# Staging the last V groups of a load phase in free buffers, and running four projection groups on the first weight half-piece

## The chip, the cores and the metric

The kernel runs on 1 core of one Trainium2 chip. The metric is device time in microseconds (us) of one execution; smaller is better. The time before was 859.42 us, the median of 3 runs (859.0 to 860.41). The span that a profile shows is about 1.7 us shorter than the time of the same run.

Engines are named as the profile names them: PE is TensorE (matmul), PEld its weight loads, ACT is ScalarE, DVE is VectorE, POOL is GpSimd, SP is SyncE, which issues nearly all DMAs here. "L463" is line 463 of the kernel. The change adds three lines early in the file, so that L699 of before is L702 of after, L512 is L515, L656 is L659, and so on.

## The reference, cut to what matters

A segment-recurrent attention layer over 64 segments, and then a gated MLP. Only the attention's loop and its weights matter here.

```python
for s in range(n_seg):                       # 64 segments of 32 rows, strictly one after another
    h = concat([mem, x[s]])                  # 8 memory rows + 32 rows
    q, k, v = h @ Wq, h @ Wk, h @ Wv         # 512 -> 32 heads x 128
    p = softmax(mask(q @ k.T * scale))
    o = (p @ v) @ Wo                         # needs every row of Wo
    mem = o[:8]                              # next segment's memory
    outs.append(o[8:])
... x + attention, then layernorm, gelu, spatial gating, output projection
```

The kernel computes what does not depend on the memory ahead of the loop: the projections Q, K and V of some rows of x, for whole chunks of 16 segments ("chunk 0", "chunk 1", ...). Chunks 0 and 1 are done in a load phase, while the weights arrive: 4 MB each of Wq, Wv, Wk and Wo. Then step 0 of the loop starts, then step 1, and so on, with no slack between the steps. For this document the load phase ends at about 54 us, and step 1 starts at about 64 us.

## The kernel before

Operations are recorded in program order. Each names the tokens (tiles) that it reads and writes, and a scheduler derives the semaphore waits: a write to a token waits for all readers of its old contents, and a DMA that stores a tile is such a reader. Each engine is given its own operations in the recorded order.

Weights come in pieces of eight heads (1 MB). The first piece of Wq is cut in two halves, so that PE can start sooner:

```python
def load_w(mi, hq):                          # mi 0, 1, 2: Wq, Wk, Wv; hq: piece 0..3
    ...
    if mi == 0 and hq == 0:
        cm = c0 + 4 * DH
        sp(lambda e, c0=c0: e.dma_start(ws[:, :, c0:cm], wr[:, :, c0:cm]), writes=["W0"])
        c0 = cm
    sp(lambda e: e.dma_start(ws[:, :, c0:c1], wr[:, :, c0:c1]), writes=[("W", mi, hq)])
```

A Q/K group `i` of a chunk is 16 matmuls of 128x128 into one PSUM bank; `hhs` names which quarter groups to run (L463). The V groups are L498. Their eviction (ACT or DVE) writes a staging buffer, which SP then stores to DRAM (`vext_d`):

```python
def qkx_mm(ck, i, bank, hhs=range(4)):
    ...
    for hh in hhs:
        wt = "W0" if i < 2 and hh < 2 else ("W", mi, q // 2)
        for dc in range(DC):
            pe(... e.matmul(ps[:, bank, hh * 128:(hh + 1) * 128], lhsT=ws[...], rhs=hTe[:, ck % 3, dc, :], ...),
               reads=[("hTe", ck % 3, dc // 2), wt], writes=[PB(bank)])

def vx_evac(ck, n, bank, eng="act"):
    if ck == 1 and n < 4:
        t, tok = (hbuf, xo)[n // 2][:, n % 2, :], [(("h", "xo")[n // 2], n % 2)]
    elif ck < 2:
        t, tok = part[:, n, :], [("part", n, 0), ("part", n, 1)]
    else:
        t, tok = Vs[:, 0, :], [("Vs", 0)]
    ...                                      # ACT or DVE: PSUM bank -> t
    sp(lambda e: e.dma_start(dst, t...), reads=tok, writes=[("vext", ck, n)])
```

So V groups 4 to 7 of chunk 1 use the same four buffers (`part` 4 to 7) as those of chunk 0, and their evictions wait until those stores have been done.

The start of the load phase, and its end:

```python
for hp in range(2):                          # start: chunk 0 on both halves of piece 0, then chunk 1
    for i in range(2):
        qkx_mm(0, i, 2 + i, (2 * hp, 2 * hp + 1))
    if hp == 0:
        xe_halves(1, 1, (0, 1))              # x transposes of chunk 1
qkx_evac(0, 0, 2, "act")
qkx_evac(0, 1, 3, "dve")
for i in range(2):
    qkx_mm(1, i, 4 + i)
    qkx_evac(1, i, 4 + i, ("act", "dve")[i])
...
for i in range(2, 8):                        # rest of Q
    for ck in range(2):
        start_group(qkx_mm, qkx_evac, ck, i)
...                                          # V groups of chunk 0, V groups 0..3 of chunk 1, load_wo(0)
load_wo(1)
for j in range(2):
    load_vx(j)                               # reads vext_d back: waits for stores of chunk 0
for i in range(8, 12):                       # first half of K
    ...
for n in range(4, 8):
    start_v(1, n)                            # V groups 4..7 of chunk 1
    if n % 2 == 1:
        load_wo(n // 2)                      # the third and the last Wo piece
for i in range(12, 16):                      # second half of K
    ...
```

`start_group` cycles through four PSUM banks. In a step the output product reads all of Wo, and `V_evac` writes the tile `V_sb`:

```python
def Wo(cbs, bank, d0, d1):                   # L699
    for c, b in cbs:
        for g in range(4):
            h = 16 * b + 4 * c + g
            pe(... rhs=w_o[:, h, d0:d1] ..., reads=[("cT", c, b), ("Wo", h // 8)], writes=[PB(bank)])

def V_evac(b, eng, gs=(0, 4)):               # L654 (ACT), L656 (DVE)
    dst, src = V_sb[:, b, 128 * gs[0]:128 * gs[1]], ps[...]
    tok = [("V", b, g) for g in range(*gs)]
    ...
```

## Time and profile before

| what | value | from |
|---|---|---|
| time | 859.42 us (859.0 to 860.41, 3 runs) | runs |
| PE busy | 845.2 us, 98% of the span | page, busy times |
| first V matmul (start of V groups) | 22.86 us | PE timeline |
| step 0 starts / step 1 starts | 54.46 / 64.69 us | PE timeline |
| Wo pieces 2, 3, 4 (counted from 1) landed | 51.66 / 58.01 / 62.79 us | completion records of the DMAs |

From the page of the kernel before, the busy times of the span, and the two DMA rows over 40 equal slices of it (21.5 us each; a digit is tenths of the DMA engines' time):

```profile
PE 845.2 (98%) x22497; PEld 427.6 (50%) x18920; DVE 506.4 (59%) x1312; ACT 471.7 (55%) x1359; POOL 156.3 (18%) x423
...
DMA  8983222213041211322241313243231690032101
GB/s 303 373 254 73 71 73 74 65 42 86 26 93 32 77 37 49 82 67 58 69 86 44 81 40 97 68 84 71 47 69 39 192 280 3 1 111 89 46 13 41
```

PE bounds the whole. But the first three slices, some 64 us, are also full of DMA. That is where both of the idle times that the change aims at lie. The busy times by stretch show them (columns: stretch, its length, busy us and instructions of each engine, granted clock, DMA share, GB/s):

```profile
35.00:54.00 19.00, 17.64 (x314) 15.40 (x313) 7.19 (x10) 6.61 (x10) 7.88 (x32) 1.00 0.95 306
54.00:64.00 10.00, 9.63 (x309) 5.08 (x251) 5.86 (x15) 6.03 (x18) 1.55 (x4) 1.00 0.75 242
```

PE lacks 19.00 - 17.64 = 1.36 us between 35 and 54 us. The PE timeline names the gaps (columns: start, duration, engine, line, operation, count; in brackets the idle time before the group and what ended it):

```profile
6.83 1.19 PE L463 MATMUL f_ps<-f_hTe,f_arena 128*128 128x128 bf16 x16 [0.16 <-ACT f_hTe L443]
7.85 0.39 PE L408 MATMUL f_ps<-f_ident,f_xn 128*128 128x128 bf16 x4
9.29 13.65 PE L463 MATMUL f_ps<-f_hTe,f_arena 128*128 128x128 bf16 x240 [1.05 <-DMA f_arena<-in_A_Wq_dram]
...
45.67 1.07 PE L463 MATMUL f_ps<-f_hTe,f_arena 128*128 128x128 bf16 x16
48.10 6.43 PE L463 MATMUL f_ps<-f_hTe,f_arena 128*128 128x128 bf16 x112 [1.36 <-DVE f_part L512]
54.46 0.40 PE L289 MATMUL f_ps<-f_arena,f_hT 128*32 128x512 bf16 x4
...
60.84 0.27 PE L290 MATMUL f_ps<-f_arena,f_hT 128*32 128x256 bf16 x1 [0.37 <-issue]
...
62.46 1.86 PE L699 MATMUL f_ps<-f_arena,f_cT 128*32 128x256 bf16 x56
```

The gap before 9.29 waits for the second half of the first weight piece, the gap before 48.10 for a bank that DVE had not yet emptied.

Why DVE was late is in the list of waits of the first 75 us (columns: who, for what, us in total, times, longest):

```profile
ACT f_part L510 <- DMA vext_d<-f_part: 5.3, 2, 3.1
DVE f_part L512 <- DMA vext_d<-f_part: 4.7, 2, 4.4
```

Both evictions waited for older stores out of `part`. And the SP timeline shows what sets the end of the Wo loads: SP stands at the read-back of V (`f_Vx`) from 45.70 to 50.07, and issues the last Wo piece at 53.72.

```profile
45.70 4.37 SPq L520 DMA_DIRECT2D f_Vx<-vext_d  x4
...
52.05 0.47 SPq L823 DMA_DIRECT2D f_arena<-in_A_Wo_dram  x1
...
53.72 0.57 SPq L823 DMA_DIRECT2D f_arena<-in_A_Wo_dram  x1
```

That last piece landed at 62.79, and step 0's Wo matmuls (L699), which need it, run from 62.46.

### The profile page before, as it was taken

To read this page: it belongs to the slowest core of one execution; us is meant where nothing else is said; L and a number is where in the kernel's file an instruction comes from. 1 tells how busy PE (TensorE), PEld (TensorE's weight loads), DVE (VectorE), ACT (ScalarE), POOL (GpSimd) and SP (SyncE) were. 2 spreads that over 40 slices of the span, in tenths; PEclk is the share of its full clock that TensorE was granted. 3 is DMA by queue.
4 is the path that set the end of the run, shared out by engine and by line. 5 is a ranking of instruction groups with operands and counts; after the bars stand their busy time and mean duration, and the time that the engine had idled before them with its cause. 6 is when DMAs were issued, how large, how long until landed. Compare 5 with 4: busy or idle time off the path is not lost.

```text
span 859.1 us, 45449 instructions
## 1 busy us (share of the span) xinstructions
PE 845.2 (98%) x22497; PEld 427.6 (50%) x18920; DVE 506.4 (59%) x1312; ACT 471.7 (55%) x1359; POOL 156.3 (18%) x423
## 2 busy tenths in 40 slices
PE   8999999999999999999999999999999999999997
PEld 8664445454444544445444454444544444444443
DVE  3546666666666666666666666666665564463443
ACT  3445666666666666666666666666666655400000
POOL 0711212121212112121211212121111132100000
PEclk9999999999999999999999999999999999999999
DMA  8983222213041211322241313243231690032101
GB/s 303 373 254 73 71 73 74 65 42 86 26 93 32 77 37 49 82 67 58 69 86 44 81 40 97 68 84 71 47 69 39 192 280 3 1 111 89 46 13 41
DMA packets 114713, 75.25 MB, mean 88 GB/s; under 512 B 70728, under 2 KB 100560, under 8 KB 114512
## 3 DMA queue, kind: packets, MB, share of 16 engines
q1 hardware_dynamic: 114224, 72.06, 30.6%
q8 instruction: 164, 2.69, 1.3%
q14 instruction: 37, 0.30, 0.1%
q10 hardware_dynamic: 288, 0.20, 0.1%
HBM read 39.46 MB, written 20.58 MB: 70 GB/s over the span
## 4 chain that ended last, share of the span: by engine, by line
PE 96%; DMA 2%; DVE 1%; issue 0%; SPq 0%; ACT 0%; DVEq 0%
PE f_ps L289 30%; PE f_ps L699 13%; PE f_ps L290 13%; PE f_ps L1148 11%; PE f_ps L749 3%; PE f_ps L498 3%; PE f_ps L463 3%; PE f_ps L664 3%; PE f_ps L1222 3%; PE f_ps L1110 3%; PE f_ps L613 3%; PE f_ps L1141 3%; PE f_ps L593 1%; PE f_ps L670 1%; DMA f_arena<-in_A_Wq_dram 1%; DMA vext_d<-f_part 1%
## 5 line engine op out<-in xcount | busy, mean ns | idle before, releaser
L289 PE MATMUL f_ps<-f_arena,f_hT 128*32 128x512 bf16 (+1 forms) x5120 | 352.9, 337 | 1.1
L290 PE MATMUL f_ps<-f_arena,f_hT 128*32 128x256 bf16 (+1 forms) x3072 | 214.6, 308 | 0.4 <-issue 0.4
L289 PEld LDWEIGHTS f_ps<-f_arena,f_hT 128*32 128x32 bf16 x5120 | 120.5, 96 | 169.0 <-issue 86.0
L557 ACT ACTIVATE f_Tst<-f_ps 128x512 bf16<-128x512 f32 (+1 forms) x320 | 149.8, 510 | 57.1 <-PE f_ps L289 53.4
L699 PE MATMUL f_ps<-f_arena,f_cT 128*32 128x256 bf16 x4096 | 130.0, 274 | 1.3 <-ACT f_cT L684 1.1
L636 POOL TENSOR_TENSOR f_E_sb<-f_R_sb,f_E_sb 128x64 bf16<-128x64 f32 x128 | 48.0, 375 | 374.4 <-ACT f_R_sb L628 374.4
L565 DVE STREAM_TRANSPOSE f_QT<-f_Tst 128x256 uint32<-128x256 uint32 x128 | 57.1, 446 | 94.5 <-ACT f_Tst L557 94.5
L699 PEld LDWEIGHTS f_ps<-f_arena,f_cT 128*32 128x32 bf16 x4096 | 90.2, 94 | 35.3 <-ACT f_cT L684 22.9
L1148 PE MATMUL f_ps<-f_arena 128*128 128x512 bf16 x448 | 100.6, 379 | 0.0
L656 DVE TENSOR_SCALAR f_V_sb<-f_ps 128x512 bf16<-128x512 f32 (+1 forms) x128 | 70.6, 552 | 40.9 <-PE f_ps L289 40.9
L686 DVE TENSOR_SCALAR f_cT<-f_ps 128x160 bf16<-128x160 f32 x256 | 65.1, 317 | 36.4 <-PE f_ps L670 36.4
L711 ACT ACTIVATE f_part<-f_ps 128x256 bf16<-128x256 f32 x128 | 49.2, 384 | 59.2 <-PE f_ps L699 56.0
L684 ACT ACTIVATE f_cT<-f_ps 128x160 bf16<-128x160 f32 x256 | 57.1, 309 | 36.9 <-PE f_ps L670 36.9
L1148 PEld LDWEIGHTS f_ps<-f_arena 128*128 128x128 bf16 x448 | 43.7, 98 | 52.8
L565 DVE STREAM_TRANSPOSE f_KT<-f_Tst 128x128 uint32<-128x128 uint32 (+1 forms) x192 | 66.0, 356 | 2.7
L624 ACT ACTIVATE f_R_sb<-f_ps 128x160 f32<-128x160 f32 x128 | 39.0, 304 | 33.6 <-PE f_ps L290 26.5
L1154 DVE TENSOR_TENSOR f_arena<-f_ps,f_arena 128x512 f32<-128x512 f32 x28 | 19.3, 690 | 54.4 <-PE f_ps L1148 52.4
L606 ACT ACTIVATE f_E_sb<-f_ps 128x224 bf16<-128x224 f32 x128 | 45.7, 357 | 0.0
L632 DVE TENSOR_TENSOR f_E_sb<-f_R_sb,f_E_sb 128x160 bf16<-128x160 f32 x128 | 44.8, 350 | 0.0
L628 ACT ACTIVATE f_R_sb<-f_R_sb 128x160 f32<-128x160 f32 x128 | 42.6, 333 | 2.0
L749 PE MATMUL f_ps<-f_arena,f_cTx 128*32 128x512 bf16 x512 | 40.6, 380 | 0.0
L289 PE MATMUL f_ps<-f_arena,f_hTe 128*32 128x512 bf16 x512 | 39.2, 382 | 0.0
(116 smaller groups left out, 1023.0 us busy)
## 6 DMA issues: line engine op xcount, KB each, us to landing
wT_d<-f_wst SPq DMA_DIRECT2D x32, 256.0 KB, 3.7
f_arena<-wT_d SPq DMA_DIRECT2D x32, 256.0 KB, 4.6
f_arena<-in_A_Wv_dram SPq DMA_DIRECT2D x4, 1024.0 KB
f_arena<-in_A_Wk_dram SPq DMA_DIRECT2D x4, 1024.0 KB, 15.7
f_arena<-in_A_Wo_dram SPq DMA_DIRECT2D x4, 1024.0 KB
f_Vx<-vext_d SPq DMA_DIRECT2D x128, 32.0 KB
f_arena<-in_A_Wq_dram SPq DMA_DIRECT2D x3, 1024.0 KB
vext_d<-f_Vs SPq DMA_DIRECT2D x16, 128.0 KB
```

What stands on the lines that cost most here:

```text
L289: return e.matmul(out, lhsT=lhsT, rhs=rhs, start=start, stop=stop, skip_group_check=True, tile_position=pos)
L290: return e.add_instruction(mybir.InstMatmult(name=nc.get_next_instruction_name(), engine=mybir.EngineType.PE, ins=[e.lower_ap(rhs), e.lowe ...
L557: act(lambda e: e.activation(out=st_.rearrange("p (hp i r) -> p hp i r", i=32, r=2), in_=ps[:, bank, 0:64 * np_].rearrange("p (hp r i) -> ...
L565: dve(lambda e: e.transpose(out=dst, in_=src), reads=tok, writes=[(nm, b, k) for k in halves(b, p0, np_)])
L636: pool(lambda e: e.tensor_tensor(out=ev, in0=rv, in1=ev, op=ALU.mult), reads=[("R", b), ("Ex", b)], writes=[("Ex", b)])
L656: dve(lambda e: e.tensor_scalar(out=dst, in0=src, scalar1=VSC, scalar2=None, op0=ALU.mult), reads=[PB(bank)], writes=tok)
L684: act(lambda e: e.activation(out=dst, in_=src, func=ACT.Copy, scale=UNSC), reads=[PB(PVB[c])], writes=tok)
L686: dve(lambda e: e.tensor_scalar(out=dst, in0=src, scalar1=UNSC, scalar2=None, op0=ALU.mult), reads=[PB(PVB[c])], writes=tok)
L699: pe(lambda e, h=h, g=g, i=i, b=b, c=c: e.matmul(ps[32 * g:32 * g + 32, bank, 0:d1 - d0], lhsT=cTh[:, i, 8:40], rhs=w_o[:, h, d0:d1], star ...
L711: act(lambda e: e.activation(out=part[:, s % 8, d0:d1], in_=ps[:, bank, 0:d1 - d0], func=ACT.Copy), reads=[PB(bank)], writes=[("part", s % ...
L749: pe(lambda e, h=h, g=g, i=8 * qr + bg: e.matmul(ps[32 * g:32 * g + 32, WXB, :], lhsT=cTx[:, rb % 2, i, :], rhs=w_o[:, h, :], start=(i < 4 ...
L1148: pe(lambda e: e.matmul(ps[:, bank, 0:TB], lhsT=z2[:, sc, fb * 128:(fb + 1) * 128], rhs=wTb[tb % 2][:, :, sc, :], start=(sc == 0), stop=(s ...
```

## The change

It has two parts. (a) At the start, both chunks run their first two groups on the first half piece (`hhs` 0 and 1), with the x transposes of chunk 1 between, and only then the second half: PE gets 16 more matmuls before it needs the second half. (b) V groups 4 to 7 of chunk 1 are staged in `Vs` and `V_sb`, which no store is reading then, so their evictions need not wait.

```diff
     def vx_evac(ck, n, bank, eng="act"):
         if ck == 1 and n < 4:
             t, tok = (hbuf, xo)[n // 2][:, n % 2, :], [(("h", "xo")[n // 2], n % 2)]
-        elif ck < 2:
+        elif ck == 1:
+            t = (Vs, V_sb)[n // 2 - 2][:, n % 2, :]
+            tok = [("Vs", n % 2)] if n < 6 else [("V", n % 2, g) for g in range(4)]
+        elif ck == 0:
             t, tok = part[:, n, :], [("part", n, 0), ("part", n, 1)]
 ...
-    for hp in range(2):
+    qkx_mm(0, 0, 2, (0, 1))
+    xe_halves(1, 1, (0, 1))
+    qkx_mm(0, 1, 3, (0, 1))
+    for i in range(2):
+        qkx_mm(1, i, 4 + i, (0, 1))
+    for ck in range(2):
         for i in range(2):
-            qkx_mm(0, i, 2 + i, (2 * hp, 2 * hp + 1))
-        if hp == 0:
-            xe_halves(1, 1, (0, 1))
-    qkx_evac(0, 0, 2, "act")
-    qkx_evac(0, 1, 3, "dve")
-    for i in range(2):
-        qkx_mm(1, i, 4 + i)
-        qkx_evac(1, i, 4 + i, ("act", "dve")[i])
+            qkx_mm(ck, i, 2 + 2 * ck + i, (2, 3))
+            qkx_evac(ck, i, 2 + 2 * ck + i, ("act", "dve")[i])
```

No work is added or removed, and the order in which SP issues DMAs is the same.

## The prediction

> **What bounds the kernel.** Over the whole span TensorE does: the page has PE busy 98% and PE 96% of the chain that ended last, clock 0.9 or better in every slice. In the first 62 us a second limit runs beside it: windows from 10 to 50 us show DMA share about 1.05 and 334 to 385 GB/s. Weights land in issue order ([...] the trace agrees: 1 MB pieces land one after another, 2.7 us apart). PE waits there for data that no reordering of PE brings sooner.
>
> **What the change does.** It adds and removes no work; SyncE's issue order stays.
>
> (a) Start. PE waits 1.05 us, 8.24 to 9.29, for the rest of the first weight piece (PE timeline). The change puts 16 matmuls of chunk 1 there, about 0.9 us (240 took 13.65 us). But the matmuls after need the second 1 MB piece, whose semaphore is full at 11.94 us. Before, the matmul with that wait was already held a little: evictions come every 0.89 us, but after 0.97 at 12.25, and a new run of weight loads starts at 11.98. After, PE has 32 matmuls (1.8 us) left at 9.29, finishes near 11.1, and waits 0.9 us. Gain at 12 us: about 0.
>
> (b) V groups 4 to 7 of chunk 1. Their evictions waited for older stores out of the same buffers (list of waits: ACT 5.3, DVE 4.7 us on DMA vext_d<-f_part), and PE idled 1.36 us before 48.10 for a bank. With Vs and V_sb as staging this goes; PE reaches step 0 near 53.1 instead of 54.46. But step 0 needs all four pieces of Wo. The last lands at 62.79, and PE got there at 62.75: its weight loads pause until 62.84. That landing hangs on SyncE's issue order and the queue: Vx loads wait for stores landing at 48.21, then stores, Wo piece 3 issued at 52.05 (lands 58.01), piece 4 at 53.72. None of that waits for what the change makes earlier. So PE arrives near 61.4 and waits about 1.35 us. Step 0's V evictions now wait for the last two staged stores (58.45, 58.84) and are wanted near 58.3 and 59.2: up to 0.2 us, hidden under the Wo wait.
>
> **Sum.** 0.9 + 1.36 = 2.3 us of visible idle is removed (0.27%); I expect 0 to 0.2 us to survive, as both idles lie ahead of a later deadline set by DMA. From 63 us on both kernels should run alike.
>
> **Predicted: 859.3 us**, 8 in 10 between 858.2 and 860.3 (three runs of before spread 1.4 us). Chances: faster by over 2% 0.005, within 2% 0.99, slower by over 2% 0.005.
>
> **What would show it.** Right: the PE gap before 9.29 shrinks to 0.2 us and one of about 0.9 ends near 11.95; no ACT or DVE wait on vext_d stores between 43 and 48 us; step 0 starts near 53.1; then over 1 us of idle in its Wo matmuls, ending near 62.85; step 1 starts near 64.7 in both. Wrong: step 1 near 63.3 ((b) kept, about 858.0) or 62.4 (both kept, 857.1).
>
> **What would make it wrong.** The last Wo piece landing earlier, if SyncE or the queue goes faster once the stores' data is ready earlier; landing times shifting by some tenths; or the staged stores landing later than step 0 wants V_sb, by more than the Wo wait hides.

## The result, and the profile after

| | median us | lowest to highest | runs |
|---|---|---|---|
| before | 859.21 | 858.67 to 860.41 | 4 |
| after | 859.13 | 858.80 to 859.79 | 4 |

The ratio after/before is 0.9998, with a 95% interval of 0.9981 to 1.0015: the same. Ratios in this document are the mean time of one kernel's runs over that of the other's runs of the same rounds, so they are not quite the ratio of the medians quoted.

The busy times by stretch, after:

```profile
35.00:54.00 19.00, 19.00 (x343) 16.04 (x331) 7.80 (x11) 7.16 (x10) 7.82 (x32) 1.00 0.96 299
54.00:64.00 10.00, 8.93 (x304) 4.69 (x248) 5.74 (x16) 5.79 (x18) 1.40 (x4) 1.00 0.73 239
```

The gap between 35 and 54 us is gone (19.00 of 19.00), and 10.00 - 8.93 = 1.07 us of idle time stands between 54 and 64 us, where there had been 0.37. PE's timeline after:

```profile
7.20 0.51 PE L463 MATMUL f_ps<-f_hTe,f_arena 128*128 128x128 bf16 x6 [0.28 <-DVE f_hTe L445]
7.54 0.39 PE L408 MATMUL f_ps<-f_ident,f_xn 128*128 128x128 bf16 x4
7.77 7.16 PE L463 MATMUL f_ps<-f_hTe,f_arena 128*128 128x128 bf16 x119
15.43 7.38 PE L463 MATMUL f_ps<-f_hTe,f_arena 128*128 128x128 bf16 x129 [0.49 <-DMA f_arena<-in_A_Wq_dram]
...
45.54 7.32 PE L463 MATMUL f_ps<-f_hTe,f_arena 128*128 128x128 bf16 x128
52.79 0.40 PE L289 MATMUL f_ps<-f_arena,f_hT 128*32 128x512 bf16 x4
...
59.48 0.27 PE L290 MATMUL f_ps<-f_arena,f_hT 128*32 128x256 bf16 x1 [0.69 <-issue]
...
61.10 0.51 PE L702 MATMUL f_ps<-f_arena,f_cT 128*32 128x256 bf16 x11
61.99 1.48 PE L702 MATMUL f_ps<-f_arena,f_cT 128*32 128x256 bf16 x45 [0.37 <-DMA f_arena<-in_A_Wo_dram]
```

Read it from the top. The wait before 9.29 is gone, but a new one stands at 15.43, for the third 1 MB piece of Wq; the first V matmul comes at 22.73 instead of 22.86. The group at 45.54 now runs its 128 matmuls without the gap in the middle, and step 0 starts at 52.79, 1.67 us earlier than before. Then that lead shrinks: the "issue" gap is 0.69 us instead of 0.37, and the Wo matmuls break off for 0.37 us until the last Wo piece has landed (61.94). Step 1 starts at 63.80, 0.89 us earlier than before in this pair of profiles; the timed runs show no such difference.

The waits of the first 75 us, after, which answer to those shown of before:

```profile
PE f_ps L290 <- issue: 0.7, 1, 0.7
...
PEld f_ps L702 <- DMA f_arena<-in_A_Wo_dram: 0.6, 1, 0.6
...
DVE f_V_sb L659 <- DMA vext_d<-f_V_sb: 0.5, 1, 0.5
```

No eviction waits for a store out of `part` any more. In their place stand three shorter waits, all in step 0: the issue gap, the wait for Wo, and a wait of DVE for a staged store out of `V_sb`.

In the chain that ended last, SP and the Wo load now stand where PE's own work stood before (start, duration, what):

```profile
49.72 0.46 SPq L517
...
52.92 9.02 DMA f_arena<-in_A_Wo_dram
...
61.99 1.48 PE f_ps L702 x45
```

So the idle time has moved to where DMA sets the pace. Three things could be holding step 0 there, and the profile alone does not separate them: the last Wo piece, the staged stores, and whatever "issue" is.

### The profile page after: what moved, and what is told of

Its sections match the earlier page's. It is cut to its first block, busy times and chain, and to the rows that moved or that the text cites. A ratio compares the mean times of both kernels' runs of the same rounds, so it can differ in the third digit from the quotient of the medians.

```text
span 858.1 us, 45452 instructions
## 1 busy us (share of the span) xinstructions
PE 844.5 (98%) x22504; PEld 426.0 (50%) x18920; DVE 506.2 (59%) x1312; ACT 471.3 (55%) x1359; POOL 156.1 (18%) x423
## 3 DMA queue, kind: packets, MB, share of 16 engines
q8 instruction: 164, 2.69, 1.3%
## 4 chain that ended last, share of the span: by engine, by line
PE 94%; DMA 3%; DVE 1%; SPq 1%; issue 0%; ACT 0%
PE f_ps L289 30%; PE f_ps L702 13%; PE f_ps L290 13%; PE f_ps L1150 11%; PE f_ps L752 3%; PE f_ps L498 3%; PE f_ps L1224 3%; PE f_ps L667 3%; PE f_ps L1112 3%; PE f_ps L616 3%; PE f_ps L1143 3%; PE f_ps L463 2%; PE f_ps L596 1%; DMA f_arena<-in_A_Wq_dram 1%; DMA f_arena<-in_A_Wo_dram 1%; PE f_ps L673 1%
```

## The experiments

### What "issue" is

Before the experiments, one reading of the traces. Take PE's matmuls and weight loads in their order of start and number them; the first is number 2, as the trace has two instructions of PE's sequencer before it. In every execution that has the "issue" gap of step 0 it falls between number 1984 and number 1985, and when there is a second one, between 2240 and 2241; later ones can be seen before 2753 and 3265. These numbers are multiples of 256 apart. The page counts "q8 instruction: 164, 2.69" as packets and MB on a DMA queue of its own: 2.69 MB over 164 packets is 16 KB each, and PE's 41417 matmuls and weight loads (22497 and 18920 on the page of before) over 164 packets are 253 to a packet, near the 256 between the gaps. Where there is a gap at number 1985, it ends 1.23 to 1.41 us after such a packet has ended (before: packet 58.51 to 59.48, PE resumes at 60.84; after: 57.28 to 58.25, PE resumes at 59.48). From these figures the gap is read here as PE waiting for its next page of 256 instructions; the profile itself names no releaser but "issue".

The packet starts 2.3 us (before) and 2.75 us (after) after PE has entered the page ahead of it, while Wo pieces are moving; on the next six, quieter pages of before it is 0.6 to 1.3 us (for example: page entered at 64.56, packet at 65.89; 73.39 and 74.18).

In the experiments "stall" is the time from the start of number 1984 to that of number 1985, with 0.65 us before and 0.97 us after. (The page's 0.37 and 0.69 are shorter, because they count from the modelled end of the matmul before.) Likewise "Wo wait" is the time at the first matmul that needs the last Wo piece (number 2128): 0.65 us after. The table below leaves out the second stall, from number 2240 to 2241, just before step 1's first instruction: it is 0.35 us before, 0.12 after, 0.74 in a_only and after_vxlate, 0.47 in b_only and after_nowo3, 0.19 in after_again, 0.20 in before_again, and nothing in the others.

### The theories

- **Deadlines (the prediction).** Both idle times stood ahead of later DMA deadlines: (a) ahead of the second and third piece of Wq, (b) ahead of the last piece of Wo. Removing them moves the wait.
- **Rival 1, stores.** The staged stores out of `V_sb` hold step 0's V evictions, and that is what takes the lead.
- **Rival 2, instruction page.** PE's next page of instructions arrives late while the Wo pieces are moving, and that takes it.
- **Rival 3, nothing is lost.** The gain is there, about 1 us, and too small to be seen in the spread of the times.

All the runs together, in us. V0 is the start of the first V group (its first matmul or weight load, as for the other starts, so they can be a few hundredths off the timeline lines); "before" in the timed columns is that of the same rounds.

| kernel | V0 | step 0 starts | stall | Wo wait | step 1 starts | median us / before | ratio (95%) |
|---|---|---|---|---|---|---|---|
| before | 22.88 | 54.47 | 0.65 | 0.14 | 64.66 | 859.21 | |
| after | 22.74 | 52.80 | 0.97 | 0.65 | 63.80 | 859.13 / 859.21 | 0.9998 (0.9981 to 1.0015) |
| a_only | 23.87 | 54.32 | 1.21 | 0 | 65.28 | 860.82 / 861.56 | 0.9997 (0.9984 to 1.0010) |
| b_only | 24.01 | 54.06 | 0.48 | 0 | 64.02 | 861.65 / 861.56 | 1.0004 (0.9986 to 1.0021) |
| after_nowo3 | 22.64 | 52.69 | 1.48 | 0 | 63.64 | 860.89 / 861.56 | 0.9990 (0.9976 to 1.0004) |
| after_vxlate | 22.76 | 52.81 | 1.86 | 0 | 64.41 | 861.21 / 861.56 | 0.9988 (0.9972 to 1.0005) |
| after_wohalf | 21.96 | 52.01 | 0.00 | 0 | 61.64 | 859.43 / 861.41 | 0.9975 (0.9953 to 0.9996) |
| before_wohalf | 22.42 | 54.13 | 0.00 | 0 | 63.76 | 860.67 / 861.41 | 0.9984 (0.9963 to 1.0006) |
| after_woearly | 22.42 | 52.63 | 0.94 | 0 | 64.55 | 862.17 / 861.41 | 1.0013 (0.9989 to 1.0036) |
| after_again | 24.04 | 54.09 | 0.42 | 0 | 63.94 | 860.41 / 861.41 | 0.9988 (0.9968 to 1.0009) |
| after_third | 21.98 | 52.03 | 1.58 | 0.56 | 63.56 | 859.97 / 860.51 | 0.9990 (0.9973 to 1.0008) |
| before_again | 21.77 | 53.67 | 0.26 | 0 | 63.35 | 861.26 / 860.51 | 1.0006 (0.9989 to 1.0024) |
| after_split | 22.04 | 52.20 | 1.39 | 0.75 | 63.74 | 859.84 / 860.51 | 0.9985 (0.9964 to 1.0006) |

In the experiments each kernel has 6 runs, and before has 11 on the same chip. The start times are those of the one profiled execution of each.

### a_only: the new start, the old staging

```diff
 (after, with vx_evac as in before)
-        elif ck == 1:
-            t = (Vs, V_sb)[n // 2 - 2][:, n % 2, :]
-            tok = [("Vs", n % 2)] if n < 6 else [("V", n % 2, g) for g in range(4)]
-        elif ck == 0:
+        elif ck < 2:
```

> Only the reordered start, V groups staged as before. Deadline theory (each idle lies ahead of a later DMA landing): the PE gap before the rest of weight piece 1 shrinks from 1.05 to below 0.3 us, a new gap of 0.6 to 0.9 us opens before the second piece lands, PE reaches the groups on that piece at the landing, and the time is that of before within 0.3 us. Rival (the idle is truly saved, the timing was too coarse to show it): 0.9 us faster, no new gap. Rival (saved but lost again much later in the steps): the first step starts 0.9 us earlier and the loss shows after 75 us.

The time is the same (0.9997). But the trace differs from what was expected at the start: V0 came at 23.87, a microsecond later than before. The PE timeline of a_only shows why:

```profile
8.55 15.38 PE L463 MATMUL f_ps<-f_hTe,f_arena 128*128 128x128 bf16 x248
...
47.96 6.43 PE L463 MATMUL f_ps<-f_hTe,f_arena 128*128 128x128 bf16 x112 [0.23 <-DVE f_part L512]
```

The 248 matmuls took 15.38 us without a wait. In after_third, the unchanged changed kernel, the same 248 took 14.10 us. The matmul starts in the trace show 4 or 5 per half microsecond (about 107 ns apart) from 8.5 to 11 us in a_only, where after has 7 to 9 (about 56 ns). That is PE's clock, and the clock column shows it: 0.50 of full speed in a_only, 1.00 in after (first a_only, then after; the clock is the third figure from the right):

```profile
8.50:11.00 2.50, 2.50 (x26) 2.50 (x24) 0.29 (x1) 0.38 (x1) 0.00 (x0) 0.50 1.05 405
8.50:11.00 2.50, 2.50 (x47) 2.42 (x44) 0.71 (x1) 1.01 (x2) 0.00 (x0) 1.00 1.05 396
```

The granted clock of a_only was full from 4.6 us on and at half from 8.0 to 11.4; that of b_only and after_again from 8.3 to 11.7. The half clock struck a_only, b_only and after_again, with and without (a), so the runs give no sign that it is of the change's making; but it spoils a_only as a test of (a). What it teaches is that the start of V varies by over 2 us (21.77 to 24.04) between executions, more than the 1.05 us that (a) aims at. And because PE came late, the wait for the `part` stores was only 0.23 us in place of 1.36: the slack of that wait absorbed the late start.

### b_only: the old start, the new staging

```diff
 (before, with vx_evac as in after)
-        elif ck < 2:
+        elif ck == 1:
+            t = (Vs, V_sb)[n // 2 - 2][:, n % 2, :]
+            tok = [("Vs", n % 2)] if n < 6 else [("V", n % 2, g) for g in range(4)]
+        elif ck == 0:
```

> Only the staging of chunk 1's V groups 4 to 7, start as before. Deadline theory: the waits of ACT and DVE on older stores vanish, step 0 starts 1.4 us earlier (about 53.1), PE waits in step 0's Wo matmuls until the last Wo piece lands (0.4 to 1.4 us, by when it lands: 61.9 to 62.8), and the time is that of before to 0.9 us less, following that landing. Rival (truly saved): 1.4 us faster, no wait for Wo.

The waits for `vext_d<-f_part` are gone, and the time is the same (1.0004). Step 0 started at 54.06 rather than near 53.1, since this execution also had the stretch at half clock (V0 at 24.01). No matmul waited for Wo, against the expectation: the last piece landed at 61.87, and PE came to it at 62.13. Yet step 1 started at 64.02. Against after (V0 at 22.74, step 1 at 63.80) V0 is 1.27 us later and step 1 only 0.22.

### after_nowo3: the change, but step 0 does not need the last Wo piece

Heads of the last piece read the piece before it in step 0. This is wrong arithmetic; the output still passed the comparison with the reference, whose tolerance this one step does not exceed.

```diff
+def Wo(cbs, bank, d0, d1, s=1):
                 h = 16 * b + 4 * c + g
+                if s == 0 and h >= 24:
+                    h -= 8
```

> The changed kernel, but step 0 reads the third Wo piece where it should read the last one: wrong result on purpose, same instructions and same DMA. Deadline theory: no wait for the last Wo piece in step 0, so step 1 starts at about 63.2 to 63.5, against 63.8 to 64.7 before, and the time is 0.5 to 1.4 us below the changed kernel. Rival (the saved time was lost to the new V_sb and Vs waits or to instruction fetch, or later): the time is that of the changed kernel.

A miss. The Wo wait is gone, as it must be: PE passed number 2128 at 61.75, and the last piece landed only at 62.38, so the edit spared this execution about 0.6 us (an estimate, the difference of the two). But step 1 started at 63.64, only 0.16 us before that of after, and the time did not change (0.9990). The rest is in the PE timeline:

```profile
59.89 0.27 PE L290 MATMUL f_ps<-f_arena,f_hT 128*32 128x256 bf16 x1 [1.21 <-issue]
```

The page stall was 1.48 us, where that of after was 0.97. It comes before the Wo matmuls in PE's order, so the edit can't have lengthened it; it differs from execution to execution, and a second one of 0.47 us followed. DVE also waited 1.7 us for staged stores, and no wait of PE for it shows. So the wait for the last Wo piece is real, but it is not the whole of what takes the lead: the deadline theory in its plain form falls here.

### after_vxlate: the change, and the read-back of V after the last Wo piece

SP no longer stands at the read-back before it issues the stores and the Wo pieces.

```diff
     load_wo(1)
-    for j in range(2):
-        load_vx(j)
 ...
         if n % 2 == 1:
             load_wo(n // 2)
+    for j in range(2):
+        load_vx(j)
```

> The changed kernel with the four first Vx loads issued after the last two Wo pieces rather than before them. Deadline theory: SyncE no longer holds the Wo pieces behind stores that land at 48 us; the last Wo piece lands near 58 to 59 instead of 61.9 to 62.8; no Wo wait; step 1 starts near 63.2; 0.9 to 1.4 us faster than before, result correct. Rival (bandwidth alone sets the landing, order does not matter): last Wo piece still after 61 us, time unchanged. Rival (Vx too late): a new PE wait of over 0.5 us in step 0 for Vx.

Also a miss. The last Wo piece was complete at 60.91 (the first of its 16 landing records is at 56.89, the last 4 us later), so no matmul waited for it; the V evictions waited for no store. Both the Wo theory and rival 1 would have PE run free. It did not:

```profile
60.39 0.27 PE L290 MATMUL f_ps<-f_arena,f_hT 128*32 128x256 bf16 x1 [1.58 <-issue]
```

The page packet ran from 57.99 to 59.14, and PE resumed at 60.39. Step 1 started at 64.41. Here the page stalls alone (1.86 us and another 0.74 at number 2241) ate nearly the whole lead: step 0 started 1.66 us earlier than in before, step 1 0.25.

### after_wohalf and before_wohalf: no third and fourth Wo load at all

Both kernels, with every use of Wo pieces 3 and 4 reading pieces 1 and 2 (wrong arithmetic) and 2 MB less to load.

```diff
-                h = 16 * b + 4 * c + g      # in Wo; likewise in WoX_mm
+                h = 4 * c + g
 ...
-        if n % 2 == 1:
-            load_wo(n // 2)
```

> The changed kernel without the last two Wo loads (2 MB less); all Wo matmuls read the first two pieces: wrong result on purpose, same PE work. The first set showed that step 0's stall lies at a fixed place in PE's instruction stream, 256 instructions apart from the next such stall, about 1.3 us after the end of a 16 KB packet on the instruction queue. Fetch theory: those packets start late (2.2 to 3.5 us after PE enters the page before) because the Wo data are in the way; here they start within 1.4 us, the stall at that place is below 0.2 us, PE waits for no Wo, step 0 lasts 9.8 to 10.0 us (11.0 in the changed kernel), and the saving of the staging survives: step 1 starts 1.2 to 1.5 us before that of the matching kernel with the old staging. Rival (the fetch delay has nothing to do with the Wo loads): stall still 0.5 us or more. Rival (V_sb waits are the main loss): DVE waits on the staged stores remain and step 0 still lasts over 10.5 us.

> The kernel before with the same removal of the last two Wo loads: wrong result on purpose. It gives the base for the run above. Fetch theory: the stall of 0.65 us at the page edge vanishes, step 0 lasts 9.8 to 10.0 us against 10.23; step 1 starts near 64.3 if the start is undisturbed; time about 0.4 us below before, and 1.2 to 1.5 us above the run above. Rival (both kernels gain the same): the two runs end equal.

These two runs decide most, though with one profile of each. Without the last two Wo loads the stall was 0.00 us in both, step 0 took 9.63 us in both, and step 1 started at 61.64 with the change and at 63.76 without. The gap of before was still there in before_wohalf, and no gap in step 0 in either, as the two PE timelines show (first before_wohalf, then after_wohalf):

```profile
47.77 6.43 PE L463 MATMUL f_ps<-f_hTe,f_arena 128*128 128x128 bf16 x112 [1.48 <-DVE f_part L512]
...
61.68 1.73 PE L699 MATMUL f_ps<-f_arena,f_cT 128*32 128x256 bf16 x56
```

```profile
44.76 7.32 PE L463 MATMUL f_ps<-f_hTe,f_arena 128*128 128x128 bf16 x128
...
59.56 1.73 PE L702 MATMUL f_ps<-f_arena,f_cT 128*32 128x256 bf16 x56
```

Of the 2.12 us between them at step 1, 0.46 were there at V0, and 1.66 came after it, where the two kernels differ in the staging alone. The times differ by 1.24 us (859.43 and 860.67), within the expectation, but their ranges overlap (857.82 to 860.65, 859.03 to 861.73), so the traces carry this point and not the times. The instruction packet for number 1985 now started 0.3 and 0.8 us before PE entered the page ahead of it, instead of 1.9 to 3.4 us after, as in all the others. So (b) does remove 1.4 to 1.7 us of idle time from the chain, and what takes it back in the real kernel comes with the last two Wo loads: as data that step 0 needs, and by delaying the page of instructions. The staged stores out of `V_sb` landed earlier too (53.98 and 54.34, instead of 57.41 and 59.30 in after), so this pair does not part the three; after_vxlate, where nothing waited for Wo or for a store, shows that the page alone is enough.

### after_woearly: the change, and the Wo pieces issued before the read-back and the staged stores

```diff
-    load_wo(1)
+    for hq in (1, 2, 3):
+        load_wo(hq)
     for j in range(2):
         load_vx(j)
 ...
-        if n % 2 == 1:
-            load_wo(n // 2)
```

> The changed kernel with the last two Wo pieces issued right behind the second, before the first Vx loads and the staged stores; result correct. Deadline theory: SyncE no longer leaves a hole in the DMA stream at 50 to 54 us; the last Wo piece lands at 56 to 58 us; no wait for it. Fetch theory: the instruction packets of step 0 still meet DMA traffic until about 58 us, so a stall of 0.3 to 1.2 us stays; step 1 starts near 63.0 to 63.6, 0.3 to 0.8 us before the changed kernel. Rival (staged stores, now behind Wo, land after step 0 wants V_sb): new DVE waits of over 0.5 us and no gain.

Rival 1 is right for this order. With Wo ahead of them, the last two staged stores landed only at 60.11 and 60.46, and DVE, which wants to write `V_sb`, waited. From the DVE timeline:

```profile
60.21 0.69 DVE L659 TENSOR_SCALAR f_V_sb<-f_ps 128x512 bf16<-128x512 f32 x1 [3.10 <-DMA vext_d<-f_V_sb]
```

The last Wo piece landed at 59.08, a microsecond later than expected, and nothing waited for it. Step 0 took 11.92 us, the longest of all, and step 1 started at 64.55. The time was 0.1% longer, inside the interval. So in the order of after, with the Wo piece last, PE waited for that piece (0.65 us), and in this order, with the stores last, for what the stores held up: number 2010 came 1.46 us after the one before it.

### after_again, after_third and before_again: the kernels unchanged

No edit; these are repeats on the chips of the experiments.

> The changed kernel once more, for the spread of its landings and of its stalls from run to run, and as the base of this set. Deadline theory: last Wo piece between 61.5 and 63 us, step 1 at 63.5 to 64.8, sum of page-edge stall and Wo wait in step 0 at 1.0 to 1.6 us, time equal to before within 0.5 us. Rival (the 0.9 us that the first profile showed at step 1 is a real gain): step 1 again at 63.8 or earlier and about 0.9 us faster than before over the rounds.

> The changed kernel a third time. Pinning theory (step 1 hangs on the Wo stream and on the instruction packet behind it, not on PE's arrival): step 1 starts at 63.6 to 64.0 again, wherever the V groups started; time 0.3 to 0.9 us below before in the mean of the rounds. Full-loss theory as predicted (nothing survives): step 1 at 64.4 or later and equal time. Full-gain rival: step 1 at 63.0 or earlier and 2 us faster.

> The kernel before, profiled and timed as a variant: tells what two equal kernels differ by, and gives a second profile for the places that pin it. Deadline theory: the first matmul on the second weight piece starts 0.1 us after that piece lands (or later, if PE's clock ramped late); step 0 starts 1.3 to 1.7 us later after the first V group than in the changed kernel (31.6 against 30.05 us) unless PE came to the V groups late; step 1 starts at 64.4 to 65.3. Time equal to before within 0.5 us.

The changed kernel's step 1 started at 63.94 and 63.56, with V0 at 24.04 and 21.98: 2.06 us apart at V0, 0.38 at step 1. That fits the pinning by DMA. In after_third, which came early, the stall was 1.58 us and the Wo wait 0.56; in after_again, which came late, 0.42 and 0, less than the 1.0 to 1.6 expected. The unchanged kernel's step 1 started at 63.35 in before_again, after 64.66 in the first profile, and not at the 64.4 to 65.3 expected: a miss. V0 was 1.11 us earlier there, so its lead was not lost, unlike that of the changed kernel. The last Wo piece did not hold it either (landed at 61.43, PE there at 61.51), and the `part` wait was 1.67 us.

before_again against the rest of before, the same kernel, gave 1.0006. Its ratio and that of after_third (0.9990) have intervals that overlap widely. What remains of the span after step 1 has started also varies, from 793.7 us (a_only: 859.0 - 65.28) to 796.9 us (b_only: 860.9 - 64.02), so that half a microsecond at step 1 can't be read off the times. In the repeats the changed kernel's median lies 0.5 and 1.0 us under that of before; both intervals contain 1. Rival 3 in a weak form, a gain of at most about 1 us, is neither shown nor refuted.

### after_split: the change, and the second weight piece in two halves as well

```diff
-        if mi == 0 and hq == 0:
+        if mi == 0 and hq < 2:              # tokens "W0", "W1"
 ...
+    for i in range(2, 4):                   # first halves of groups 2 and 3, both chunks
+        for ck in range(2):
+            qkx_mm(ck, i, 2 + 2 * (i - 2) + ck, (0, 1))
```

(and the second halves run where the whole groups ran.)

> The changed kernel with the second 1 MB weight piece loaded in two halves, and the four groups on it run their first half first, as the change does for the first piece; result correct. Deadline theory for the start: PE no longer waits for the whole second piece, so the V groups start 0.4 to 0.9 us earlier than in the changed kernel with the same clock ramp (22.0 to 22.3 against 22.7), step 0 starts as much earlier, but step 1 stays at 63.6 to 64.0 and the time is that of the changed kernel. Rival (the V start is bound by PE alone): V groups start as before.

It was meant as a test of (a) and as a candidate for a better kernel. The second piece's halves landed at 10.21 and 11.66, and V0 came at 22.04, as expected. But after_third, without the split, had it at 21.98 in the same session, so nothing shows that the split brought it. Step 1 started at 63.74, as in the other staged kernels, with a stall of 1.39 us and a Wo wait of 0.75. Its median (859.84) is the lowest of those that compute the right result in its session, but the interval of its ratio contains 1. No version here beats both kernels by an amount that the runs can show.

## Why the prediction was right

**The size was right**: 859.3 us was predicted, 859.13 measured; "0 to 0.2 us to survive" was the sum, and the ratio is 0.9998. That it agrees to 0.2 us is partly luck, as four runs of before alone lie 1.74 us apart. The reason given, idle time ahead of later DMA deadlines, holds for (a); for (b) it holds in kind, but the wait for the last Wo piece was less than half of that forecast, and longer stalls for the page of instructions, not forecast, took part of the lead (0.97 us where it had been 0.65). Point by point:

- **(a), "But the matmuls after need the second 1 MB piece".** Right. The first matmul on that piece started 0.11 us after the piece had landed, in both kernels (before 12.05 after 11.94; after 11.25 after 11.14). The wait of about 0.9 us "ended near 11.95" was not seen in that form: the piece landed earlier this time, and PE then waited 0.49 us for the third piece, which landed at 15.38. V0 moved by 0.14 us. The repeats agree: V0 came 10.98 us after the landing of the second piece with the old start (before_again: 21.77 after 10.79) and 11.11 after it with the new one (after_third: 21.98 after 10.87). What the prediction did not consider is that PE's clock moves this start: in the three executions with a stretch at half clock V0 came at 23.87 to 24.04, in the others at 21.77 to 22.88.
- **(b), the waits on stores go and step 0 starts near 53.1.** Right: it started at 52.80.
- **(b), "So PE arrives near 61.4 and waits about 1.35 us" for the last Wo piece.** The arrival was right (61.34), the wait was mis-sized: 0.65 us. The piece landed at 61.94, 0.85 us earlier than in before; the prediction took one landing time as fixed, and it varies by that much between executions.
- **What filled the difference** was not in the prediction: the stall for the next page of instructions. Its text does not name the 0.37 us of "issue" that stood in step 0 before. In the definition used here the stall was 0.65 us before, 0.97 and 1.58 us in the two early executions of after, 0.00 without the last two Wo loads. Among the nine executions that keep these loads and the order around them it was 0.97 to 1.58 us where step 0 started by 52.80, and 0.26 to 1.21 where it started later, so an early PE tends to wait longer, but the packet's own time varies as well.
- **The staged stores, "up to 0.2 us, hidden".** Mis-sized: the second of them landed at 59.30, DVE waited 0.5 us; it was hidden, under the page stall. after_woearly shows that it stops being hidden when the stores land a microsecond later.
- **"Step 1 starts near 64.7 in both."** Wrong by 0.9 us for after (63.80; 63.94 and 63.56 in the repeats). But the old staging itself ranges from 63.35 (before_again) to 65.28 (a_only), so it varies between executions by more than the 1.4 us that the forecast turns on, and the prediction's "Wrong" line, 63.3, would have been met by the unchanged kernel in one of its two profiles.

**What stays open.** Which of the DMA engines fetches the page, and what it stands behind: the packet for number 1985 started 0.03 to 1.2 us after the third Wo piece had landed in eight executions that keep the order of these DMAs and load that piece (before 58.51 after 58.01; after 57.28 after 57.00), which fits a fetch queued behind that piece. But in after_split, which keeps that order too, it started 0.45 us before that piece had fully landed (56.96 and 57.41), the traces do not say which engine ran a packet, and no run here moved that piece alone. Open too is whether the half to one microsecond by which after's medians lay lower in the repeats is real (in the first comparison it was 0.08).

## What to carry to other kernels

An idle time ahead of a later deadline is worth only the slack up to that deadline, so before removing a wait, look up when the next transfers that the same work needs will land, and allow for their jitter (here the last Wo piece landed at 62.79 in before and at 61.94 in after, with the same order of DMAs). Where the DMA queues are busy while that work runs (here a DMA share of 0.75 from 54 to 64 us of before), count the packets of the instruction queue among those transfers: here "issue" gaps 256 instructions apart, at 1985 and 2241, were their sign, and the first of them was 0.97 to 1.58 us where step 0 started by 52.80, and 0.26 to 1.21 where it started later (the nine executions with these loads in this order). To learn whether a removed wait is worth anything, take the suspected later deadline away in both kernels (as the two runs without the last Wo loads do) and compare; and run the kernels again unchanged, since here one kernel's step 1 moved by 1.3 us from one execution to the next.

## Further figures of these traces

- **The page of instructions.** Number 1985 came without a stall (0.00 us) in the two kernels without the last two Wo loads; with those loads PE stood still for 0.26 to 1.86 us there. Without them a stall can still show elsewhere: 0.41 us at number 2753 in before_wohalf. From the end of the packet to the next instruction it took 1.23 to 1.41 us where there was a stall at 1985. One page of 256 instructions lasted PE 4.0 us in step 0 (56.20 to 60.19 before).
- **The spread of one load.** Each 1 MB load left 16 landing records, as many as the page counts DMA engines. The first and the last were 1.9 us apart for the last Wo piece before (60.91 and 62.79), 2.9 us for the third Wq piece after (12.48 and 15.38), and 4.0 us in after_vxlate. PE's wait for that Wq piece after ended at 15.43, just behind the last of them (the fifteenth was at 13.43), so the spread was part of the deadline.
- **The clock at the start.** The profile's clock column reads 1.00 from 0 to 5 us of before, while the 44 matmuls from 1.07 on took 4.67 us, 106 ns each. The first clock record of that trace is at 5.4 us, and from there on the matmuls start about 55 ns apart (5.41, 5.46, 5.52); in after it is at 3.9 us, and the starts go from about 107 to 56 ns apart there too. So before the first record the pace has to be read from the matmuls' starts; the later stretch at half clock does stand in the column (0.50 in a_only).
